# Reordered loads, more staging buffers and finer segment transfers in the forward and backward pass of a strided convolution stem

## The chip, the cores and the metric

The kernel runs on one core of a Trainium2 chip. The metric is the device time of one execution in microseconds (us). The engines are TensorE (PE, with its weight loads as PEld), VectorE (DVE), ScalarE (ACT), GpSimd (POOL) and SyncE (SP); in this kernel SP issues all loads and POOL all stores.

## The reference

The forward pass is a one-dimensional convolution with 31 taps and stride 2, a normalization over the sequence for each channel, and a GELU. The backward pass follows from it for a given `grad_out`.

```
B, T, D, K = 2, 16000, 256, 31            # x [B,T,D], w [K,D,D], all bfloat16
L = (T - K) // 2 + 1                      # 7985
h = sum over i of  x[:, i:i+2*L:2, :] @ w[i]
mu, var over l for each (b, d)
h = (h - mu) / sqrt(var + 1e-5) * gn_gamma + gn_beta
out = gelu(h, approximate=True)
outputs: out, d_x, d_w, d_gamma, d_beta   # the last four by jax.vjp with grad_out
```

Three products of the same size make nearly all of the arithmetic: the forward convolution, the gradient of x, and the gradient of w.

## The kernel before, in words

The kernel is written with a tile framework. Its scheduler places the instructions of each engine from a model of their durations and from the number of buffers in each pool; each engine then executes its own list strictly in order. A buffer that is still being read or stored makes the next writer wait, and everything behind that writer on its engine waits too.

Phase 1, `conv_forward(b)`, runs over 16 tiles of 512 output positions (`LT`) for each of the two batch entries. For each tile, four transposing loads (two halves of the channels, two parities of the stride) bring x with channels on partitions into `xt` buffers, of which there are 16. Then 124 matmuls (L186: 31 taps, two input halves, two output halves) accumulate into two PSUM tiles `acc_f`; ScalarE copies the result into `hT` and sums it and its square (L195, L202). The weights `w_sb` are loaded once at the top, in two transfers (L133), one for each half of the input channels.

Beside the second entry's convolution, the elementwise work of the first one runs, cut into items that are handed out step by step (`elementwise_items`, `run_items`): `bwd_load_go` loads `grad_out` transposed into `gT` (L280, eight large transposing loads), `elementwise_forward` makes the GELU output, `bwd_pass1` multiplies `gT` by the GELU's derivative and sums it, `bwd_pass2` applies the normalization's gradient to `gT`. The forward output and the finished `gT` are turned back to rows in `transpose_and_store`: two PE transposes into a PSUM tile `pt` (L236, two buffers), a ScalarE copy into a staging row (L238), a store by POOL (L239) to the output or to the scratch tensor `gh_dram`. The staging pool `stg` has four buffers for `row` and four for `xrow`.

Phase 2, `conv_backward_x(b)`, makes the gradient of x: for each parity and each chunk of 128 rows, up to 32 matmuls (L451: 16 taps, two halves of d) into `acc_x`, five PSUM buffers, a ScalarE copy to `xrow` (L460) and a store (L461). It needs the weights transposed: `wT_sb` (L480) takes the place of `w_sb` in the same memory, so its load starts when the last forward matmul is done. The elementwise work of the second entry runs beside the first entry's part.

Phase 3 makes the gradient of w. The sequence is cut into 125 blocks of 64 positions, one on each partition (`NG` = 125). Each of four segments (two entries, two halves of a block) holds 32 rows of the gradient per partition in `gseg` and 93 rows of x in `xg`, two buffers each. Both are loaded in three pieces, bounded by gradient rows 8, 20 and 32:

```
s_bounds = [0, min(SH, 8), min(SH, 20), SH]
...
r_hi = min(RW, 2 * (s_hi - 1) + K)
```

`gseg` rows are one load (L542), x rows one load (L550) on 125 partitions, or 124 and a single row (L555) where the last block of x runs out. The taps are taken in groups of eight (`groups`); a group sweeps all 32 rows, 16 matmuls a row (L567), into eight PSUM tiles, and VectorE adds them to the fp32 sum `gw_acc` (L579, L581). At the very end each of 62 half-taps is cast to bfloat16, in turn by VectorE (L587) and ScalarE (L589), and stored by POOL (L590), with four staging buffers `wrow`. The memory of phase 3 is that of phases 1 and 2, so its first load waits for the last work of phase 2.

Of the kernel before, what the change touches and what calls it, by code (L numbers as in the profile page):

```python
# [9 lines left out]
ALU = mybir.AluOpType  # L10
AX = mybir.AxisListType
FP32 = mybir.dt.float32
BF16 = mybir.dt.bfloat16
# [11 lines left out]
def kernel(  # L25
# [13 lines left out]
    nc = tc.nc  # L39
    P = 128  # L40
    B, T, C = x.shape
    K, C2, D = w.shape
    assert C2 == C and C % P == 0 and D % P == 0
    S = 2
    L = (T - K) // S + 1
    assert tuple(grad_out.shape) == (B, L, D)
    NCC = C // P
    NDD = D // P
# [72 lines left out]
    with ExitStack() as ph12:  # L121
# [2 lines left out]
        xtp = ph12.enter_context(tc.tile_pool(name="xtp", bufs=16, side="right"))  # L124
        temps = ph12.enter_context(tc.tile_pool(name="temps", bufs=2, side="right"))
        otp = ph12.enter_context(tc.tile_pool(name="otp", bufs=4, side="right"))
        stg = ph12.enter_context(tc.tile_pool(name="stg", bufs=4, side="right"))
        ps_mm = ph12.enter_context(tc.tile_pool(name="ps_mm", bufs=5, space=bass.MemoryType.PSUM))
        ps_tr = ph12.enter_context(tc.tile_pool(name="ps_tr", bufs=2, space=bass.MemoryType.PSUM))

        w_sb = wpool.tile([P, NCC, K, D], BF16, name="w_sb", tag="w")
        for cc in range(NCC):
            dma_in.dma_start(  # L133
                out=w_sb[:, cc, :, :],
                in_=w[:, cc * P:(cc + 1) * P, :].rearrange("k c d -> c k d"),
            )

        hT = [None] * B
        gT = [None] * B
        wT_holder = [None]  # L140

        def conv_forward(b):
            hT_b = big.tile([P, NDD, GW], BF16, name=f"hT{b}", tag="big")
            hT[b] = hT_b
            for lt in range(NLT):
                l0 = lt * LT
                N = min(LT, L - l0)
                xt = {}
                for cc in range(NCC):
                    for par in range(2):  # L150
                        mmax_p = (K - 1 - par) // 2
                        need = N + mmax_p
                        Wp = ((need + 15) // 16) * 16
                        avail = NU[par] - l0
                        t_xt = xtp.tile([P, LT + 16], BF16, name="xt", tag="xt")
                        if Wp <= avail:
                            dma_in.dma_start_transpose(
                                out=t_xt[:, 0:Wp],
                                in_=x[b, bass.ds(2 * l0 + par, Wp, step=2), cc * P:(cc + 1) * P],
                            )  # L160
                        else:
                            W16 = (need // 16) * 16
                            if W16 > 0:
                                dma_in.dma_start_transpose(
                                    out=t_xt[:, 0:W16],
                                    in_=x[b, bass.ds(2 * l0 + par, W16, step=2), cc * P:(cc + 1) * P],
                                )
                            rem = need - W16
                            if rem > 0:
                                with nc.allow_non_contiguous_dma(reason="xT tail rows"):  # L170
                                    dma_in.dma_start(
                                        out=t_xt[:, W16:need],
                                        in_=x[b, bass.ds(2 * (l0 + W16) + par, rem, step=2),
                                              cc * P:(cc + 1) * P].rearrange("u c -> c u"),
                                    )
                        xt[(cc, par)] = t_xt
                accs = [ps_mm.tile([P, LT], FP32, name="acc_f", tag="acc") for dd in range(NDD)]
                total = K * NCC
                n = 0
                for i in range(K):  # L180
                    par = i % 2
                    m = i // 2
                    for cc in range(NCC):
                        rhs = xt[(cc, par)][:, m:m + N]
                        for dd in range(NDD):
                            nc.tensor.matmul(  # L186
                                accs[dd][:, 0:N],
                                lhsT=w_sb[:, cc, i, dd * P:(dd + 1) * P],
                                rhs=rhs,
                                start=(n == 0),  # L190
                                stop=(n == total - 1),
                            )
                        n += 1
                for dd in range(NDD):
                    nc.scalar.activation(  # L195
                        out=hT_b[:, dd, PADL + l0:PADL + l0 + N],
                        in_=accs[dd][:, 0:N],
                        func=ACT.Copy,
                        accum_out=hsum_part[b][:, dd, lt:lt + 1],
                    )  # L200
                    junk = temps.tile([P, LT], BF16, name="junk_a", tag="junk_a")
                    nc.scalar.activation(  # L202
                        out=junk[:, 0:N],
                        in_=accs[dd][:, 0:N],
                        func=ACT.Square,
                        accum_out=hsq_part[b][:, dd, lt:lt + 1],
                    )
                yield
# [169 lines left out]
        def elementwise_items(b):  # L378
# [1 line left out]
            p1 = bwd_pass1(b)  # L380

            def loader():
                bwd_load_go(b)
                yield "A"

            items.append((loader(), 0.5, False))
# [77 lines left out]
        def n_bx_chunks():  # L464
            return sum(_cdiv(NU[par], P) for par in range(2))

        for _ in conv_forward(0):
            pass
        ew_items = [None] * B
        for b in range(1, B):  # L470
            items = new_sched(elementwise_items(b - 1), lag=1)
# [4 lines left out]
                    run_items(items, (k + 1) / nsteps)  # L476
            run_items(items, 1.0)
        wT_sb = wpool.tile([P, NDD, K, C], BF16, name="wT_sb", tag="w")
        for dd in range(NDD):
            dma_in.dma_start_transpose(  # L480
                out=wT_sb[:, dd, :, :].rearrange("p k c -> p (k c)"),
                in_=w[:, :, dd * P:(dd + 1) * P].rearrange("k c d -> (k c) d"),
            )
        wT_holder[0] = wT_sb
        last = B - 1
        items_last = new_sched(elementwise_items(last), lag=6)
# [23 lines left out]
    with ExitStack() as ph3:  # L510
        accp = ph3.enter_context(tc.tile_pool(name="accp", bufs=1))
        seg = ph3.enter_context(tc.tile_pool(name="seg", bufs=2, side="right"))
        stg3 = ph3.enter_context(tc.tile_pool(name="stg3", bufs=4, side="right"))
        ps_w = ph3.enter_context(tc.tile_pool(name="ps_w", bufs=8, space=bass.MemoryType.PSUM))
        GRP = 8
        groups = [list(range(i0, min(K, i0 + GRP))) for i0 in range(0, K, GRP)]
# [2 lines left out]
        for b in range(B):  # L519
            for h in range(NH):  # L520
# [5 lines left out]
                if nfull < NG:  # L526
                    qb0 = (g_last // 32) * 32
                    r_inv0 = max(0, max_r_last + 1)
                    nc.gpsimd.memset(xg[qb0:qb0 + 32, r_inv0:RW, :], 0.0)  # L529
                s_bounds = [0, min(SH, 8), min(SH, 20), SH]  # L530
                r_prev = 0
                for pi in range(3):
                    s_lo, s_hi = s_bounds[pi], s_bounds[pi + 1]
                    if s_hi <= s_lo:
                        continue
                    r_hi = min(RW, 2 * (s_hi - 1) + K)
                    gsrc = bass.AP(
                        tensor=gh_dram.tensor,
                        offset=gh_dram[b, SH * h + s_lo, 0].offset,
                        ap=[[SB * D, NG], [1, (s_hi - s_lo) * D]],  # L540
                    )
                    dma_in.dma_start(out=gseg[0:NG, s_lo:s_hi, :].rearrange("g s d -> g (s d)"), in_=gsrc)  # L542
                    if r_hi > r_prev:
                        if nfull > 0:
                            src = bass.AP(
                                tensor=x.tensor,
                                offset=x[b, 2 * SH * h + r_prev, 0].offset,
                                ap=[[2 * SB * C, nfull], [1, (r_hi - r_prev) * C]],
                            )
                            dma_in.dma_start(out=xg[0:nfull, r_prev:r_hi, :].rearrange("g r c -> g (r c)"), in_=src)  # L550
                        if nfull < NG:
                            nv = min(max_r_last + 1, r_hi)
                            if nv > r_prev:
# [3 lines left out]
                                    in_=x[b, t0 + r_prev:t0 + nv, :].rearrange("(o r) c -> o r c", o=1),  # L557
                                )
                        r_prev = r_hi
                for grp in groups:  # L560
                    accs = [ps_w.tile([P, NCC, D], FP32, name="acc_w", tag="accw") for _ in grp]
                    total_per_bank = SH * NCC
# [12 lines left out]
                    for ti, i in enumerate(grp):  # L575
                        dst = gw_acc[:, i, :]
                        src_ps = accs[ti][:].rearrange("p k d -> p (k d)")
                        if first_seg:
                            nc.vector.tensor_copy(out=dst, in_=src_ps)  # L579
                        else:  # L580
                            nc.vector.tensor_tensor(out=dst, in0=src_ps, in1=dst, op=ALU.add)  # L581
                first_seg = False
        for i in range(K):
            for cc in range(NCC):
                wrow = stg3.tile([P, D], BF16, name="wrow", tag="wrow")
                if (i * NCC + cc) % 2 == 0:
                    nc.vector.tensor_copy(out=wrow[:], in_=gw_acc[:, i, cc * D:(cc + 1) * D])  # L587
                else:
                    nc.scalar.copy(out=wrow[:], in_=gw_acc[:, i, cc * D:(cc + 1) * D])  # L589
                dma_out.dma_start(out=out_2[i, cc * P:(cc + 1) * P, :], in_=wrow[:])  # L590


# [28 lines left out]
```

## Time and profile before

The median of four runs is 2735.53 us (2733.92 to 2736.33).

| Engine | busy, us | share of the span of 2732.4 us |
|---|---|---|
| PE matmul | 2617.9 | 96% |
| PE weight load | 1965.3 | 72% |
| DVE | 573.2 | 21% |
| ACT | 418.1 | 15% |
| POOL | 321.4 | 12% |

| matmul group | busy, us | count |
|---|---|---|
| forward, L186 | 849.2 | 3968 |
| gradient of x, L451 | 880.5 | 7812 |
| gradient of w, L567 | 870.9 | 7936 |
| transposes, L236 (one of two rows) | 34.8 | 252 |

An engine's busy time counts the stretches in which one of its instructions ran. In lines of groups and waits, `<-` stands between what is written and what is read, or between who waits and who released it; a wait's three numbers are its total, its count and the longest. The columns of a timeline are start, duration, engine, line, operation, tiles and, in brackets, the idle time before it and who ended it. SPq is SP's queue of transfer issues. In windows, the clock that the throttle granted (1.00 is full speed), the mean share of the 16 DMA engines and GB/s stand last.

### The profile page before, as it was taken

How to read it: one execution, taken by the hardware profiler on the slowest of the kernel's cores; microseconds unless marked ns; L12 is line 12 of the kernel's file. 1: busy time of each engine (PE TensorE's matmuls, PEld its weight loads, DVE VectorE, ACT ScalarE, POOL GpSimd, SP SyncE). 2: the span in 40 equal slices, each digit the busy share in tenths (PEclk: the TensorE clock that was granted, in tenths of full speed). 3: DMA queues.
4: the chain of work that ended last, by engine and by line, in shares of the span. 5: the costliest groups of instructions: out<-in, count | busy, mean ns of one | idle time of the engine just before them, and what ended most of it. 6: DMA issues, size and time to landing. Idle time of an engine off the chain costs nothing.

```text
span 2732.4 us, 45468 instructions
## 1 busy us (share of the span) xinstructions
PE 2617.9 (96%) x20220; PEld 1965.3 (72%) x20220; DVE 573.2 (21%) x1547; ACT 418.1 (15%) x1054; POOL 321.4 (12%) x586
## 2 busy tenths in 40 slices
PE   7999999899999799999999999959999999999997
PEld 3444445344445588888888888858888888888886
DVE  0000003946470786660000000000000100010111
ACT  0101013424221544412211111100000000000000
POOL 0000000001011422224311111110000000000112
PEclk9999999999999899999999999989999999999999
DMA  4101012311122401111100000013202001100000
GB/s 100 24 17 24 16 21 41 72 24 40 24 59 49 117 29 35 34 30 59 41 20 21 19 20 21 21 63 108 78 1 100 19 1 50 69 1 1 17 17 30
DMA packets 143088, 104.92 MB, mean 38 GB/s; under 512 B 128836, under 2 KB 128870, under 8 KB 141394
## 3 DMA queue, kind: packets, MB, share of 16 engines
q1 hardware_dynamic: 124652, 65.17, 9.3%
q0 software_dynamic: 18240, 36.85, 4.5%
q8 instruction: 158, 2.59, 0.4%
q14 instruction: 38, 0.31, 0.0%
HBM read 36.04 MB, written 36.82 MB: 27 GB/s over the span
## 4 chain that ended last, share of the span: by engine, by line
PE 35%; issue 22%; POOL 6%; DVE 2%; DMA 1%; ACT 1%; POOLq 0%; ACTq 0%; SPq 0%; DVEq 0%
PE acc_w L567 26%; PE acc_x L451 9%; POOL out_dram L461 3%; POOL gh_dram L239 2%; POOL out_dram L590 1%; DMA xg<-in_x_dram 1%; ACT row L238 0%; DMA gh_dram<-row 0%; PE pt L236 0%; DVE junk_v L336 0%; DVE inner L311 0%; DVE gT L329 0%; DVE inner L257 0%; DVE gw_acc L581 0%; ACT sg L260 0%
## 5 line engine op out<-in xcount | busy, mean ns | idle before, releaser
L567 PE MATMUL acc_w<-gseg,xg 125*128 125x256 bf16 x7936 | 870.9, 273 | 30.9 <-DMA xg<-in_x_dram 30.8
L451 PE MATMUL acc_x<-wT_sb,gT 128*128 128x256 bf16 (+1 forms) x7812 | 880.5, 274 | 4.3 <-issue 4.3
L186 PE MATMUL acc_f<-xt,w_sb 128*128 128x512 bf16 (+1 forms) x3968 | 849.2, 375 | 19.8 <-DMA xt<-in_x_dram 19.8
L567 PEld LDWEIGHTS <-xg 125*128 125x128 bf16 x7936 | 777.5, 98 | 124.2 <-issue 31.3
L451 PEld LDWEIGHTS <-gT 128*128 128x128 bf16 (+1 forms) x7812 | 764.6, 99 | 92.7 <-issue 6.0
L186 PEld LDWEIGHTS <-w_sb 128*128 128x128 bf16 x3968 | 385.1, 98 | 463.5 <-issue 12.4
L461 POOL DMA_DIRECT2D out_dram<-xrow x252 | 136.3, 541 | 650.8 <-ACT xrow L460 583.7
L579 DVE COPY gw_acc<-acc_w 128x512 f32<-128x512 f32 x31 | 18.9, 680 | 841.1 <-PE acc_w L567 841.1
L460 ACT CAST xrow<-acc_x 128x256 bf16<-128x256 f32 (+1 forms) x252 | 93.1, 370 | 592.6 <-PE acc_x L451 574.0
L581 DVE TENSOR_TENSOR gw_acc<-acc_w,gw_acc 128x512 f32<-128x512 f32 x93 | 56.7, 680 | 565.0 <-PE acc_w L567 565.0
L239 POOL DMA_DIRECT2D out_dram<-row x126 | 67.9, 545 | 805.1 <-ACT row L238 792.3
L589 ACT CAST wrow<-gw_acc 128x256 bf16<-128x256 f32 x31 | 12.5, 405 | 900.3 <-DVE gw_acc L581 856.8
L195 ACT ACTIVATE hT<-acc_f 128x512 bf16<-128x512 f32 (+1 forms) x64 | 37.5, 586 | 568.6 <-PE acc_f L186 568.6
L211 DVE TENSOR_REDUCE hsum<-hsum_part 128x2 f32<-128x32 f32 x2 | 0.4, 186 | 516.4 <-ACT hT L195 516.4
L238 ACT COPY row<-pt 128x256 bf16<-128x256 bf16 (+1 forms) x252 | 86.7, 378 | 41.2 <-DMA gh_dram<-row 28.4
L590 POOL DMA_DIRECT2D out_dram<-wrow x62 | 33.4, 543 | 406.6 <-DVE wrow L587 399.1
L239 POOL DMA_DIRECT2D gh_dram<-row x126 | 67.8, 542 | 64.6 <-ACT row L238 61.2
L529 POOL MEMSET xg<- 32x7424 bf16 x2 | 12.6, 6280 | 460.2 <-PE acc_w L567 458.5
L262 DVE TENSOR_TENSOR osl<-z,sg 128x512 bf16<-128x512 bf16 (+1 forms) x64 | 25.0, 414 | 162.9 <-PE pt L236 155.9
L236 PE MATMUL pt<-ident,gT 128*128 128x128 bf16 (+1 forms) x252 | 34.8, 232 | 24.2 <-ACT row L238 23.2
L253 ACT ACTIVATE z<-z 128x512 bf16<-128x512 bf16 (+1 forms) x64 | 39.5, 620 | 118.3 <-DVE z L250 118.0
L236 PEld LDWEIGHTS <-gT 128*128 128x128 bf16 (+1 forms) x252 | 24.3, 104 | 34.9 <-issue 29.6
(74 smaller groups left out, 809.7 us busy)
## 6 DMA issues: line engine op xcount, KB each, us to landing
out_dram<-xrow POOLq DMA_DIRECT2D x248, 64.0 KB, 1.8
out_dram<-row POOLq DMA_DIRECT2D x124, 64.0 KB, 2.1
gh_dram<-row POOLq DMA_DIRECT2D x124, 64.0 KB, 1.8
gseg<-gh_dram SPq DMA_DIRECT2D x8, 750.0 KB
xg<-in_x_dram SPq DMA_DIRECT2D x4, 1500.0 KB
xg<-in_x_dram SPq DMA_DIRECT2D x4, 1488.0 KB
xg<-in_x_dram SPq DMA_DIRECT2D x2, 2812.5 KB
xg<-in_x_dram SPq DMA_DIRECT2D x2, 2790.0 KB
```

The lines of the kernel that those rows point to most:

```text
L186: nc.tensor.matmul(accs[dd][:, 0:N], lhsT=w_sb[:, cc, i, dd * P:(dd + 1) * P], rhs=rhs, start=(n == 0), stop=(n == total - 1),)
L195: nc.scalar.activation(out=hT_b[:, dd, PADL + l0:PADL + l0 + N], in_=accs[dd][:, 0:N], func=ACT.Copy, accum_out=hsum_part[b][:, dd, lt:lt ...
L236: nc.tensor.transpose(out=pt[0:M, dd, :], in_=srcs[dd][:, c0:c0 + M], identity=ident[:])
L238: nc.scalar.copy(out=row[0:M, :], in_=pt[0:M].rearrange("p k d -> p (k d)"))
L239: dma_out.dma_start(out=dram_dst[b, l0 + c0:l0 + c0 + M, :], in_=row[0:M, :])
L253: nc.scalar.activation(out=z2[:, 0:N], in_=z[:, 0:N], func=ACT.Square)
L451: nc.tensor.matmul(acc[0:Mu, 0:C], lhsT=gT_b[:, dd, PADL + u0 - m:PADL + u0 - m + Mu], rhs=wT_sb[:, dd, i, :], start=(n == 0), stop=(n == ...
L460: nc.scalar.copy(out=xrow[0:Mu, :], in_=acc[0:Mu, 0:C])
L461: dma_out.dma_start(out=out_1[b, bass.ds(2 * u0 + par, Mu, step=2), :], in_=xrow[0:Mu, :])
L567: nc.tensor.matmul(accs[ti][:, cc, :], lhsT=xg[0:NG, 2 * s + i, cc * P:(cc + 1) * P], rhs=gseg[0:NG, s, :], start=(cnt[ti] == 0), stop=(cn ...
L581: nc.vector.tensor_tensor(out=dst, in0=src_ps, in1=dst, op=ALU.add)
L590: dma_out.dma_start(out=out_2[i, cc * P:(cc + 1) * P, :], in_=wrow[:])
```

## The change

The change touches every place where loads, staging or stores stand next to the matmuls, and leaves the matmuls as they are.

- The first tile's activations are loaded ahead of the weights, and the weights come tap by tap in 31 loads.
- Activation tiles are requested three tiles ahead by a list.
- The first entry's gradient is loaded after step 8 of the first convolution.
- `stg` has 12 buffers of each kind instead of 4.
- The transposed weights come in eight loads: four groups of up to eight taps, two halves each.
- Each segment of phase 3 is loaded in six pieces, bounded by rows 4, 8, 14, 20, 26 and 32; a piece has only the x rows that the first group of taps needs, and each load is split at partition 112.
- In the last segment, VectorE writes the sum straight to a bfloat16 row, which is stored, so that the closing loop of casts goes.

```diff
-        stg = ph12.enter_context(tc.tile_pool(name="stg", bufs=4, side="right"))
+        stg = ph12.enter_context(tc.tile_pool(name="stg", bufs=12, side="right"))
...
-        for cc in range(NCC):
-            dma_in.dma_start(
-                out=w_sb[:, cc, :, :],
-                in_=w[:, cc * P:(cc + 1) * P, :].rearrange("k c d -> c k d"),
-            )
+        def load_w():
...
+            for i in range(K):
+                dma_in.dma_start(
+                    out=w_sb[:, :, i, :],
+                    in_=w[i].rearrange("(cc c) d -> c cc d", c=P),
+                )
...
+        XT_LEAD = 3
...
+        def prefetch_xt(upto_idx):
+            for idx in range(min(upto_idx + 1, len(conv_order))):
+                key = conv_order[idx]
+                if key not in xt_q:
+                    xt_q[key] = load_xt(*key)
+                    if not w_loaded[0]:
+                        load_w()
...
+                idx = conv_order.index((b, lt))
+                prefetch_xt(idx + XT_LEAD)
+                xt = xt_q[(b, lt)]
...
             def loader():
-                bwd_load_go(b)
+                if b > 0:
+                    bwd_load_go(b)
                 yield "A"
...
-        for _ in conv_forward(0):
-            pass
+        for k, _ in enumerate(conv_forward(0)):
+            if k == 8:
+                bwd_load_go(0)
...
-        for dd in range(NDD):
-            dma_in.dma_start_transpose(
-                out=wT_sb[:, dd, :, :].rearrange("p k c -> p (k c)"),
-                in_=w[:, :, dd * P:(dd + 1) * P].rearrange("k c d -> (k c) d"),
-            )
+        TG = 8
+        for i0 in range(0, K, TG):
+            i1 = min(K, i0 + TG)
+            for dd in range(NDD):
+                dma_in.dma_start_transpose(
+                    out=wT_sb[:, dd, i0:i1, :].rearrange("p k c -> p (k c)"),
+                    in_=w[i0:i1, :, dd * P:(dd + 1) * P].rearrange("k c d -> (k c) d"),
+                )
...
-        stg3 = ph3.enter_context(tc.tile_pool(name="stg3", bufs=4, side="right"))
+        stg3 = ph3.enter_context(tc.tile_pool(name="stg3", bufs=16, side="right"))
...
-                s_bounds = [0, min(SH, 8), min(SH, 20), SH]
+                s_bounds = sorted(set([0] + [min(SH, v) for v in (4, 8, 14, 20, 26)] + [SH]))
...
-                    r_hi = min(RW, 2 * (s_hi - 1) + K)
-                    gsrc = bass.AP(
-                        tensor=gh_dram.tensor,
-                        offset=gh_dram[b, SH * h + s_lo, 0].offset,
-                        ap=[[SB * D, NG], [1, (s_hi - s_lo) * D]],
-                    )
-                    dma_in.dma_start(out=gseg[0:NG, s_lo:s_hi, :].rearrange("g s d -> g (s d)"), in_=gsrc)
+                    r_hi = RW if s_hi == SH else min(RW, 2 * (s_hi - 1) + GRP)
+                    PG = (NG // 16) * 16
+                    for p0, p1 in ((0, PG), (PG, NG)):
+                        gsrc = bass.AP(
+                            tensor=gh_dram.tensor,
+                            offset=gh_dram[b, SB * p0 + SH * h + s_lo, 0].offset,
+                            ap=[[SB * D, p1 - p0], [1, (s_hi - s_lo) * D]],
+                        )
+                        dma_in.dma_start(out=gseg[p0:p1, s_lo:s_hi, :].rearrange("g s d -> g (s d)"), in_=gsrc)
...
+                        for p0, p1 in ((0, PG), (PG, nfull)):
...
-                            dma_in.dma_start(out=xg[0:nfull, r_prev:r_hi, :].rearrange("g r c -> g (r c)"), in_=src)
+                            dma_in.dma_start(out=xg[p0:p1, r_prev:r_hi, :].rearrange("g r c -> g (r c)"), in_=src)
...
+                last_seg = (b == B - 1) and (h == NH - 1)
...
-                        else:
+                        elif not last_seg:
                             nc.vector.tensor_tensor(out=dst, in0=src_ps, in1=dst, op=ALU.add)
+                        else:
+                            for cc in range(NCC):
+                                wrow = stg3.tile([P, D], BF16, name="wrow", tag="wrow")
+                                nc.vector.tensor_tensor(out=wrow[:], in0=accs[ti][:, cc, :],
+                                                        in1=gw_acc[:, i, cc * D:(cc + 1) * D], op=ALU.add)
+                                dma_out.dma_start(out=out_2[i, cc * P:(cc + 1) * P, :], in_=wrow[:])
...
-                if (i * NCC + cc) % 2 == 0:
-                    nc.vector.tensor_copy(out=wrow[:], in_=gw_acc[:, i, cc * D:(cc + 1) * D])
-                else:
-                    nc.scalar.copy(out=wrow[:], in_=gw_acc[:, i, cc * D:(cc + 1) * D])
-                dma_out.dma_start(out=out_2[i, cc * P:(cc + 1) * P, :], in_=wrow[:])
```

## The prediction

> **What bounds the kernel now.** I read the page's busy line first, then the waits of PE, then the timeline around each of the long ones. The two lines below are the busy line of the page and the matmul line of its forty slices.
>
> ```profile
> PE 2617.9 (96%) x20220; PEld 1965.3 (72%) x20220; DVE 573.2 (21%) x1547; ACT 418.1 (15%) x1054; POOL 321.4 (12%) x586
> PE   7999999899999799999999999959999999999997
> ```
>
> The reader sees that TensorE is the bound: 2617.9 of 2732.4 us. The change keeps all 20220 matmuls, so at most the other 114.5 us can go, with the time in which PE runs at half clock after a pause. The dips are where that lies: slices 1, 8, 14, 27 and 40. The waits of PE put numbers to it:
>
> ```profile
> PE pt L236 <- ACT row L238: 41.2, 28, 7.8
> PE acc_w L567 <- DMA xg<-in_x_dram: 30.8, 1, 30.8
> PE acc_f L186 <- DMA xt<-in_x_dram: 19.8, 2, 19.4
> PE acc_x L451 <- issue: 4.3, 1, 4.3
> ```
>
> That is 96.1 us in 32 waits. The last matmul starts at 2716.0, so some 16 us of tail make most of the rest. Now each place on the timeline: the start, the handover to the weight gradient, the second sweep's start, the tail.
>
> ```profile
> 1.96 6.09 SPq L133 DMA_DIRECT2D w_sb<-in_w_dram  x2
> 19.44 1.01 PE L186 MATMUL acc_f<-xt,w_sb 128*128 128x512 bf16 x2 [19.44 <-DMA xt<-in_x_dram]
> ...
> 886.63 17.57 SPq L480 DMA_TRANSPOSE wT_sb<-in_w_dram  x2
> 911.30 0.42 PE L451 MATMUL acc_x<-wT_sb,gT 128*128 128x256 bf16 x1
> ...
> 1817.33 0.34 SPq L542 DMA_DIRECT2D gseg<-gh_dram  x1
> 1817.72 0.28 SPq L550 DMA_DIRECT2D xg<-in_x_dram  x1
> 1845.34 5.07 PE L567 MATMUL acc_w<-gseg,xg 125*128 125x256 bf16 x23 [30.82 <-DMA xg<-in_x_dram]
> ...
> 2719.76 2.13 POOL L590 DMA_DIRECT2D out_dram<-wrow  x4 [36.05 <-DVE wrow L587]
> 2728.10 0.54 POOL L590 DMA_DIRECT2D out_dram<-wrow  x1 [0.29 <-ACT wrow L589]
> ```
>
> The first activations queue behind the whole weight load. At the handover PE waits 28 us for a first piece of 3.39 MB (gseg 8 rows, xg 45 rows of 512 B on 125 partitions): 121 GB/s. The windows say why it is slow (busy columns, then clock, DMA share, GB/s):
>
> ```profile
> 1821.00:1824.00 3.00, 0.00 (x0) 0.00 (x0) 0.00 (x0) 0.00 (x0) 2.84 (x1) 0.50 0.37 155
> 1833.00:1836.00 3.00, 0.00 (x0) 0.00 (x0) 0.00 (x0) 0.00 (x0) 0.00 (x0) 0.50 0.34 146
> 10.00:12.00 2.00, 0.00 (x0) 0.07 (x1) 0.00 (x0) 0.00 (x0) 0.00 (x0) 1.00 1.06 291
> ```
>
> Only a third of the 16 DMA engines moves it, while the weight load at the start keeps all busy. And behind PE's wait for row copies stand these:
>
> ```profile
> ACT row L238 <- DMA gh_dram<-row: 28.4, 32, 3.6
> ACT xrow L460 <- DMA out_dram<-xrow: 11.8, 1, 11.8
> DVE gT L329 <- DMA gT<-in_grad_out_dram: 8.8, 2, 7.1
> ```
>
> ScalarE waits for one of four staging rows to be stored, and VectorE waits for gradient transposes that arrive late.
>
> [...] 5/16 is 0.31, and the share is 0.28 to 0.37. [...] the trace's row stores land 1.8 to 2.1 us after issue. [...] after a pause PE falls to half clock[...]: 0.50 from 1821, 6 us after the last matmul, and 23 matmuls in 5.07 us after it, against 2.5 us at the mean of 0.11.
>
> **The change part by part.**
>
> *Start.* Activations first, then 31 tap loads. Two small loads end by 1.8; four transposes at 1.1 to 1.2 us each (row of L157: 1108 minimum) reach 6.5; the first tap (131 KB, 0.45 us at 291 GB/s) is issued in about 0.4 us and lands some 2 us later: first matmul at 9.2 instead of 19.44. Later taps arrive every 0.45 us and feed four matmuls (0.85 us), so PE is not starved. The next activation tiles are issued from 20.5 and land by 28, needed at about 37. Gain 10.2 us (8 to 12). The lead of 3 tiles changes nothing: the 16 buffers already let the queue run four tiles ahead.
>
> *Gradient load at step 8.* The 8.8 us VectorE wait pushes back ScalarE, whose row copies stand behind its elementwise work, and PE sits 7.8 us at 497 to 504.8, then some 4 us at half clock (2 us lost). Eight transposes of 2.4 us on the queue near 240 us hide under a lead of three tiles, 80 us. The built order has its row copies still behind elementwise work, so some small waits stay: gain 8 us (4 to 10).
>
> *Twelve staging rows, weights in eight transposes.* The built program's order now has PE issue 80 matmuls of acc_x before it needs the last weight piece; before, five. The last piece still lands near 906 (same bytes from 886.6). But ScalarE now paces: after the forward sweep's end at 888 it has 46 row copies (0.37 plus a gap, 0.40: 18.4), about 12 elementwise calls of 0.62 (7.4), 5 xrow copies (1.9), table loads and the root (2.9): 30.6 us, so the transposes end at 918.6. Before they ended at 935.9, with 34 more acc_x done (3.7 us). That is 13.6. Against it, transposes now stand one or two matmuls apart (0.13 + 0.19 us each against 0.40 on ScalarE), costing 1.4 us in the 14 before the sweep's end. ScalarE was busy only 31 of 50 us there before, so I don't trust it to run gapless: gain 10 us (3 to 15). In the second batch's burst near 1300 the denser order gives back what the rows save: 0.
>
> *xrow.* POOL stops 12 us at 1215 behind the two 2-byte-strided parameter stores; four xrow buffers fill, and PE loses 4.3 us and then 2.8 (25 matmuls in 5.5 us). Twelve buffers at one per 3.3 us are 39 us of slack: gain 6.5.
>
> *Handover.* First piece: gseg 4 rows, xg 14 rows: 1.15 MB in four DMAs[...]. At 121 × 16/5 = 387 GB/s that is 3.0 us; at the weight load's 290 it is 4.0. Four issues of 0.38, and 2 us to land: first matmul at 1822.8 (1822 to 1825.5) instead of 1845.3. Then 192 KB per step s, which PE works off in 16 × 0.11 = 1.75 us: 110 GB/s, well under the rate. Gain 22.5 (18 to 23). The half-clock start stays, as 8 us of pause is still enough for it.
>
> *Tail.* Before, adds of 0.61 each for 7 taps, then 14 casts and stores through four rows: the last issue at 2728.1, 13 us after the first add. Now 14 half-size adds (estimate 0.34 each: half of 0.61 plus a margin) feed POOL at 0.543: first issue 2715.5, last 2715.5 + 13 × 0.543 = 2722.6. Gain 5.5 (4 to 6). The extra adds in the earlier groups lie beside PE.
>
> Sum: 10.2 + 8 + 10 + 6.5 + 22.5 + 5.5 = 62.7; 2735.5 − 62.7 = 2673.
>
> **Rivals.** *R1, ScalarE and POOL take over in the transposes:* the denser order speaks for it, POOL's 0.54 per store as well; that 46 copies only take 18 us speaks against. The 18 us of the gradient load and staging parts vanish, 4 more lost: 2695. *R2, the handover stays long:* 24 to 29 small DMAs per segment on one queue[...]. If they run at the old 121 GB/s, the first piece still takes 9.5 us and lands at about 1829, and then 121 GB/s against the 110 that PE needs leaves no room, say 3 us of waits: gain 13, total 2682. *R3, everything overlaps:* ScalarE gapless, all PE waits for rows gone: 63 + 15 = 2658. *R4, slower:* tap and piece loads become serial at some 3 us each. Twenty pieces for the first group then take 60 us against the 44 PE needs, the taps 93 against 27, about 80 lost, minus the gains elsewhere: 2750. The issue durations of 0.34 us speak against it.
>
> **How the numbers follow.** Forecast 0.60, R1 0.18, R2 0.10, R3 0.08, R4 0.04. The time is the forecast's, 2673. The range takes in R2, most of R1, and the upper ends of start and transposes in the forecast and R3: 2654 to 2700. Faster 0.95, same 0.01, slower 0.04.
>
> **What would show it.** Right: first acc_f near 9; no PE wait over 3 us near 500; acc_x going from 893 on, transposes done near 919; no issue gap near 1225; acc_w 8 to 9 us after the last acc_x with a DMA share near 1; last store issued 7 us after the first. Wrong: PE waiting for row copies over 30 us in all, or acc_w stopping for gseg or xg within its first group.

## The result and the profile after

The changed kernel takes 2679.26 us (median of eight runs, 2676.4 to 2682.08) against 2735.81 us for the kernel before (twelve runs, 2733.67 to 2737.74). The ratio is 0.9794, with a 95% interval of 0.9784 to 0.9804: 56.5 us less, where 62.7 was forecast.

The busy line and the matmul line of the slices, from the page of the changed kernel:

```profile
PE 2615.0 (98%) x20220; PEld 1963.4 (73%) x20220; DVE 566.9 (21%) x1547; ACT 404.3 (15%) x1023; POOL 321.1 (12%) x586
PE   8999999999999899999999999989999999999998
```

PE does the same 20220 matmuls in nearly the same busy time (2617.9 us before). The span fell from 2732.4 to 2675.3 us, and the time that is not PE's from 114.5 to 60.3. The waits of PE in the changed kernel say what is left of it:

```profile
PE pt L262 <- ACT row L264: 15.7, 8, 4.6
PE acc_w L601 <- DMA xg<-in_x_dram: 11.0, 1, 11.0
PE acc_f L212 <- DMA w_sb<-in_w_dram: 9.8, 1, 9.8
PE acc_x L478 <- DMA wT_sb<-in_w_dram: 6.9, 6, 2.2
PE acc_x L478 <- issue: 3.5, 2, 3.0
```

The wait for row copies fell from 41.2 to 15.7, the handover from 30.8 to 11.0, the start from 19.8 to 9.8. A new row has come, the wait for pieces of the transposed weights. The gap that the profile gives to "issue", time in which PE waits for nothing that the profile shows, is still there. The places where these waits stand, on the changed kernel's timeline:

```profile
9.76 10.61 PE L212 MATMUL acc_f<-xt,w_sb 128*128 128x512 bf16 x41 [9.76 <-DMA w_sb<-in_w_dram]
...
490.83 0.37 PE L262 MATMUL pt<-ident,osl 128*128 128x128 bf16 x2 [4.63 <-ACT row L264]
...
876.44 1.15 PE L478 MATMUL acc_x<-wT_sb,gT 128*128 128x256 bf16 x5 [2.23 <-DMA wT_sb<-in_w_dram]
...
905.48 0.29 PE L262 MATMUL pt<-ident,gT 128*49 128x128 bf16 x2
...
960.68 0.37 PE L262 MATMUL pt<-ident,osl 128*128 128x128 bf16 x2 [4.56 <-ACT row L264]
...
1787.07 0.83 SPq L575 DMA_DIRECT2D gseg<-gh_dram  x2
1787.96 0.77 SPq L583 DMA_DIRECT2D xg<-in_x_dram  x2
1795.25 16.95 PE L601 MATMUL acc_w<-gseg,xg 125*128 125x256 bf16 x141 [10.99 <-DMA xg<-in_x_dram]
...
2663.41 4.72 DVE L619 TENSOR_TENSOR wrow<-acc_w,gw_acc 128x256 bf16<-128x256 f32 x14 [43.74 <-PE acc_w L601]
2664.12 7.43 POOL L621 DMA_DIRECT2D out_dram<-wrow  x14 [38.04 <-DVE wrow L619]
```

To compare traces I cut each at the start of certain matmuls (the first of a group, the 400th acc_x, and so on). The second pair of columns is a repetition of both kernels, from the experiments below, where the kernel before takes 8.6 us less. Times are us.

| stage | before | changed | before, again | changed, again |
|---|---|---|---|---|
| to the first acc_f | 19.4 | 9.8 | 19.3 | 9.5 |
| to the end of the forward sweeps | 866.9 | 861.1 | 865.9 | 863.4 |
| to the 400th acc_x | 82.3 | 68.4 | 81.2 | 66.7 |
| to the 2000th acc_x | 183.8 | 187.6 | 185.4 | 188.0 |
| to the 2800th (parameter stores) | 98.7 | 97.7 | 91.6 | 91.9 |
| to the 3400th (second row burst) | 81.1 | 77.3 | 80.2 | 77.3 |
| last acc_x to first acc_w | 31.1 | 11.3 | 30.9 | 11.0 |
| last acc_w to the end | 16.4 | 10.9 | 16.4 | 10.9 |

The stages left out (the last 4400 acc_x, the rest of phase 3) make 1.5 us together. In the first pair the gains are 9.7 at the start, 5.8 in the forward sweeps, 13.9 in the overlap behind them, of which the next stage gives 3.8 back, 1.0 at the parameter stores, 3.8 in the second burst, 19.8 at the handover and 5.5 in the tail. Two things were not in the forecast: one stage is slower than before, and the parameter-store stage, of which 6.5 us were expected, shows next to nothing.

### The profile page after: what moved, and what is told of

Read it like the earlier page. It is cut to its first block, busy times and chain, and to the rows that moved or that the text cites. A ratio compares the mean times of both kernels' runs of the same rounds, so it can differ in the third digit from the quotient of the medians.

```text
span 2675.3 us, 45553 instructions
## 1 busy us (share of the span) xinstructions
PE 2615.0 (98%) x20220; PEld 1963.4 (73%) x20220; DVE 566.9 (21%) x1547; ACT 404.3 (15%) x1023; POOL 321.1 (12%) x586
## 3 DMA queue, kind: packets, MB, share of 16 engines
q1 hardware_dynamic: 135536, 65.18, 11.3%
q8 instruction: 158, 2.59, 0.4%
## 4 chain that ended last, share of the span: by engine, by line
PE 33%; issue 16%; POOL 3%; DMA 0%; ACT 0%; DVE 0%; POOLq 0%; SPq 0%; DVEq 0%; ACTq 0%
PE acc_w L601 32%; POOL out_dram L488 3%; PE acc_x L478 1%; DMA xg<-in_x_dram 0%; POOL gh_dram L265 0%; PE pt L262 0%; ACT row L264 0%; DVE wrow L619 0%; POOLq L488 0%; POOL out_dram L621 0%; DVE gw_acc L613 0%; DMA out_dram<-xrow 0%; SPq L575 0%; POOLq L654 0%; DVEq L654 0%
## 5 line engine op out<-in xcount | busy, mean ns | idle before, releaser
L478 PEld LDWEIGHTS <-gT 128*128 128x128 bf16 (+1 forms) x7812 | 764.7, 99 | 100.1 <-issue 13.4
L615 DVE TENSOR_TENSOR gw_acc<-acc_w,gw_acc 128x512 f32<-128x512 f32 x62 | 37.8, 680 | 396.3 <-PE acc_w L601 396.3
L619 DVE TENSOR_TENSOR wrow<-acc_w,gw_acc 128x256 bf16<-128x256 f32 x62 | 20.9, 412 | 196.3 <-PE acc_w L601 196.3
L398 DVE SCALAR_TENSOR_TENSOR gT<-y,bbcoef,tq 128x512 bf16<-128x512 bf16 (+1 forms) x64 | 46.4, 727 | 0.0
L262 PE MATMUL pt<-ident,osl 128*128 128x128 bf16 (+1 forms) x252 | 30.6, 222 | 14.6 <-ACT row L264 13.4
```

The source lines that it names most:

```text
L398: nc.vector.scalar_tensor_tensor(out=gseg, in0=y[:, 0:N], scalar=bbcoef[b][:, dd:dd + 1], in1=tq[:, 0:N], op0=ALU.mult, op1=ALU.add)
L478: nc.tensor.matmul(acc[0:Mu, 0:C], lhsT=gT_b[:, dd, PADL + u0 - m:PADL + u0 - m + Mu], rhs=wT_sb[:, dd, i, :], start=(n == 0), stop=(n == ...
```

## The experiments

The study ran on three chips (0, 5 and 6 in the record, which names none for the first pair), where the kernel before takes 2725.8 to 2731.1 us. So single totals are not set against the 2679.26 above; I read the stages. Traces of the same code differ by some 3 us in the forward sweeps (860.8 to 864.3), so nothing smaller is read there.

### The two kernels again

> The changed kernel itself, beside the next two on one chip, for the comparison of their traces: a ratio to the kernel before near 0.979, as on the first chip, or up to 0.983 if the pause at the parameter stores, which differed by several us from run to run in the same code, is part of what the chips differ by.

> The kernel before itself, for its trace on this chip: 31 us at the handover, 82 us from the end of the forward sweep to the 400th matmul of acc_x, 16 us of tail, as on the first chip; the pause at the parameter stores may be shorter than 4.3 us.

The changed kernel took 2673.42 us (four runs) against 2727.24 for the kernel before, ratio 0.9805 [0.9792, 0.9819]. The kernel before, run alone, took 2725.79. Their stages are the right half of the table: everything repeats within 3 us, except the parameter-store stage. That stage is 98.7 and 91.6 us for the same code of before, 97.7 and 91.9 for the same changed code. Between the two kernels of one pair it hardly differs. The eight traces of the study that keep the old stores, on all three chips, have 91.6 to 93.1 us, so whether the 97.7 and 98.7 of the first pair belong to its chip or to chance stays open.

### The parameter stores

The forecast held that four xrow buffers filled while POOL was held up by the two stores of 256 two-byte pieces each. The changed kernel has twelve, and its timeline still shows this:

```profile
1183.16 0.72 POOL L539 DMA_DIRECT2D out_dram<-gbet_bf  x1
...
1190.75 0.37 ACT L487 CAST xrow<-acc_x 128x256 bf16<-128x256 f32 x1 [2.29 <-PE acc_x L478]
1197.57 0.37 PE L478 MATMUL acc_x<-wT_sb,gT 128*128 128x256 bf16 x1 [2.97 <-issue]
...
1198.93 0.37 ACT L487 CAST xrow<-acc_x 128x256 bf16<-128x256 f32 x1 [7.81 <-remote]
1201.73 0.54 POOL L265 DMA_DIRECT2D out_dram<-row  x1 [12.19 <-DMA out_dram<-ggam_bf]
```

After the two stores, ScalarE stands still for 7.8 us with no releaser on this core ("remote"), of which some 2.9 are its usual wait for the next chunk, and PE for 2.97 plus 0.54 us with none at all. Both go on within 1.4 us of each other, while POOL still waits. A buffer cannot be what ScalarE waits for: with one xrow every 3.3 us, twelve last 39 us. Nor can PE be out of accumulators, of which it has five: the pause of 8 us is 2.4 chunks. So I stored the two vectors as rows of 256 bytes, in the changed kernel (e1) and in the one before (e7):

```diff
...
-        dma_out.dma_start(out=out_3.rearrange("(k p) -> p k", p=P), in_=ggam_bf[:])
-        dma_out.dma_start(out=out_4.rearrange("(k p) -> p k", p=P), in_=gbet_bf[:])
...
+        pt_gb = ps_tr.tile([P, NDD, P], BF16, name="pt_gb", tag="pt")
+        nc.tensor.transpose(out=pt_gb[0:2 * NDD, 0, :], in_=gb_bf[:], identity=ident[:])
+        gb_row = const.tile([P, P], BF16, name="gb_row")
+        nc.scalar.copy(out=gb_row[0:2 * NDD, :], in_=pt_gb[0:2 * NDD, 0, :])
+        dma_out.dma_start(out=out_3.rearrange("(k p) -> k p", p=P), in_=gb_row[0:NDD, :])
+        dma_out.dma_start(out=out_4.rearrange("(k p) -> k p", p=P), in_=gb_row[NDD:2 * NDD, :])
```

> The changed kernel with the gradients of gamma and beta turned to rows by one PE transpose and stored as 256-byte rows, instead of 256 two-byte pieces each. Theory F (the two-byte stores hold up the transfers that refill the engines' instructions, so PE and ScalarE stop at once): the 3.5 us of PE idle without a releaser near 1195 and the half clock after it go, POOL no longer waits 12 us for a parameter store, the last acc_x ends 5 to 7 us earlier, total about 2673. Theory B (PE stops because its PSUM buffers or xrow buffers are full): POOL's wait also goes, so the time is the same as with F; but then the changed kernel's 12 xrow buffers should have removed the stall already. Theory N (the stall has nothing to do with these stores): 2679 and the idle stays.

> The kernel before with the parameter gradients stored as 256-byte rows. Theory F: the 4.3 us of PE idle near 1222 and the half clock after it go, 6 to 7 us in all: 2729. Rival: 2735 and the idle stays, or moves to where four xrow buffers are full.

e1 took 2673.41 us and e7 2728.61, one run each. The totals show no gain: the changed kernel's repetition took 2673.42, and the kernel before 2726.57 on e7's chip. The stage is 91.0 us in e1 and 91.3 in e7, 0.9 and 0.3 below the repetitions, so the 5 to 7 us that were expected didn't come where the pause was short to begin with.

The edit moves the stores as well as reshaping them. The built order puts the new transpose behind the last matmul of phase 2, so the rows are stored some 600 us later than the strided pieces (those start at 1182.46 and 1183.16 in the changed kernel):

```profile
1781.37 0.53 POOL L540 DMA_DIRECT2D out_dram<-gb_row  x1
```

So e1 and e7 show what happens without the strided stores in the middle of phase 2. They don't tell the form of the stores from their place. The stretch of ten microseconds after the stores, in the windows of the changed kernel and then of e1:

```profile
1190.00:1200.00 10.00, 6.50 (x52) 5.08 (x50) 0.00 (x0) 0.74 (x2) 0.00 (x0) 0.87 0.06 7
```

```profile
1190.00:1200.00 10.00, 10.00 (x94) 8.96 (x93) 0.00 (x0) 1.12 (x3) 2.85 (x6) 1.00 0.14 41
```

In the changed kernel PE loses 3.5 us and then runs below full clock, down to 0.65 in the 6 us after 1200; in e1 it works all the time at full clock, and POOL issues stores throughout. The DMA view of the same 26 us shows what else is different. First the changed kernel, then e1:

```profile
q8 instruction: 1, 0.02, 1.4%
out_dram<-xrow POOLq DMA_DIRECT2D x6, 64.0 KB, 15.4
out_dram<-row POOLq DMA_DIRECT2D x4, 64.0 KB, 14.7
```

```profile
q8 instruction: 2, 0.03, 0.6%
out_dram<-xrow POOLq DMA_DIRECT2D x8, 64.0 KB, 1.8
out_dram<-row POOLq DMA_DIRECT2D x4, 64.0 KB, 3.0
```

Behind the strided stores a row takes 14.7 to 15.4 us to land instead of 1.8 to 3.0; e1's rows of 256 bytes landed 1.6 us after issue. No run tells the mechanism. The one packet of the instruction queue took 1.4% of 16 engines for 26 us, or 5.8 us; in e1 each took 1.2 (0.6% × 16 × 26 / 2). So a late packet of this queue would explain why two engines stop together with no releaser, which is a guess: the profile names the queue, not who waits for it. The other traces support it in part. In all ten with the strided stores the instruction packet due behind them took 2.6 to 11.2 us (seven traces) or began only 25 to 26 us after the one before it, where 12 to 16 are usual (e2, e3, e4); in the four with rows none took over 1.6 there. But in five of the ten (both pairs and e5) PE goes on only 3 to 9 us after that packet has ended, and in nine of the ten POOL goes on within 2.1 us of PE. With twelve buffers the profile names nothing for ScalarE's stop in two traces and the landing of a row store in five. So whether that packet is what stops PE, or all of them wait for the traffic of the stores to pass, isn't settled.

What is shown: with the strided stores, all ten traces, the first pair's among them, have an issue wait of PE's acc_x, from 0.2 to 4.3 us, and 4.8 to 12.2 us between two of ScalarE's xrow copies behind the stores, where 3.3 are usual. With the rows at the end (e1, e7 and two later runs), none of four has an issue wait, and no two copies there are more than 4.0 us apart. The size differs from trace to trace in the same code. The number of buffers is not what decides PE's part of it: with four it is 4.3, 0.2 and 0.8 us (both traces of the kernel before and e4), with twelve 0.8 to 3.5.

### Four staging buffers, weights in two loads, gradient loaded late

Three kernels undo one part each of the changed one: four buffers again (e4), `wT_sb` in two loads (e5), the first entry's gradient loaded by the items again (e6).

```diff
-        stg = ph12.enter_context(tc.tile_pool(name="stg", bufs=12, side="right"))
+        stg = ph12.enter_context(tc.tile_pool(name="stg", bufs=4, side="right"))
```
```diff
-        TG = 8
+        TG = K
```
```diff
-                if b > 0:
-                    bwd_load_go(b)
+                bwd_load_go(b)
...
-        for k, _ in enumerate(conv_forward(0)):
-            if k == 8:
-                bwd_load_go(0)
+        for _ in conv_forward(0):
+            pass
```

> The changed kernel with 4 staging rows of each kind again. Theory S (the rows' share of the gain lies around the start of the second sweep): ScalarE waits for row stores 20 to 28 us in all again, the built order spreads the transposes wider again, the first entry's last transposes end 5 to 10 us later relative to the end of the forward sweep, total 2685 to 2690. Rival W (the weights in eight loads did it all, rows are only waited for while the weights are missing anyway): total within 2 us of 2679.

> The changed kernel with the transposed weights in two loads again. Theory W: PE has only 5 matmuls of acc_x to do before the second load lands near 893, 75 fewer than with eight loads, so 8 us are lost: total 2687. Rival S (ScalarE's row copies set the pace until 905 anyway): total within 2 us of 2679.

> The changed kernel with the first entry's gradient loaded by the elementwise list again, beside the second convolution. Theory G: VectorE waits 8 to 9 us for the gradient, ScalarE falls back, PE loses 7 to 8 us near 490 instead of 4.6, plus the half clock after it: total 2682 to 2685. Rival (the wait for row copies near 490 comes from the order of ScalarE's list and not from the load): total 2679.

| us | total | forward sweeps | to 400th acc_x | to 2000th | parameter stores | second burst |
|---|---|---|---|---|---|---|
| changed, again | 2673.4 | 863.4 | 66.7 | 188.0 | 91.9 | 77.3 |
| e4, four buffers | 2681.8 | 863.7 | 70.5 | 187.2 | 92.0 | 83.0 |
| e5, two loads | 2677.2 | 861.2 | 77.7 | 183.6 | 93.1 | 77.3 |
| e6, gradient late | 2675.0 | 865.5 | 67.5 | 187.1 | 92.3 | 77.3 |

*Rows (e4).* ScalarE's waits and PE's waits in e4, one line of each:

```profile
ACT row L264 <- DMA gh_dram<-row: 27.0, 35, 2.6
```

```profile
PE pt L262 <- ACT row L264: 27.7, 22, 4.6
```

ScalarE waits for staging rows as it did in the kernel before (28.4), against 2.3 to 2.6 us in the two traces of the changed kernel; PE waits 12 us more. Of that, 2 to 4 us are in the first burst and 5.7 in the second (83.0 against 77.3). In the parameter-store stage e4 is no slower than its neighbours, although ScalarE does wait there 10.1 us for one of four xrow: the xrow buffers are worth nothing here. The rows also decide when the first entry's transposes are done: 48.1 us after the forward sweeps in e4, 32.8 to 34.6 in the two traces of the changed kernel.

*Pieces of the transposed weights (e5).* With two loads the stage to the 400th acc_x is 9.3 to 11.0 us longer than in the two traces of the changed kernel, and the next is 4.0 to 4.4 shorter, so the eight loads are worth 5.3 to 6.6, of the 8 expected. The second number is not a cost of theirs. PE's timeline in the changed kernel has a wait of 4.56 us at 960.68 (above), in the second of the two stages. E5 has it as well, but earlier, ahead of its 400th acc_x at 948.7:

```profile
945.74 0.37 PE L262 MATMUL pt<-ident,osl 128*128 128x128 bf16 x2 [4.50 <-ACT row L264]
```

In the kernel before there are four shorter waits of 1.27 to 2.59 us between 928 and 988, 7.9 us in all, of which only the last is behind its 400th acc_x (968.6). In the changed kernel the row copy stands on ScalarE behind the second entry's elementwise chain, where a ScalarE instruction at 954.38 waited 4.66 us for VectorE. The reading is that PE now gets there before that chain is done; no run tests it. The long wait costs clock as well: 0.83 on the mean from 950 to 970.

*Gradient load (e6).* The sweeps are 1.2 to 4.7 us longer than in the traces with the early load (860.8 to 864.3), and the wait that the load was to end is back, in VectorE's waits and PE's longest:

```profile
DVE gT L355 <- DMA gT<-in_grad_out_dram: 7.9, 2, 6.6
```

```profile
PE pt L262 <- ACT row L264: 18.2, 8, 6.9
```

The longest wait is 6.9 us, where 7 to 8 were expected, against 4.6: the early load takes 2.3 us off it. The 4.6 that remain (490.83 above) are not the load's: in that stretch ScalarE's own list has two elementwise calls of 0.63 us, each waiting on VectorE (the first for 4.93 us), and then the forward tile's copies, before it comes to the row copy.

### The handover: division, piece size, number of engines

Three kernels: one load of 125 partitions instead of 112 and 13 (e2), the old three pieces but divided at 112 (e3), and a division at 100 (e9), with a DMA share of 0.56 to 0.62 in the wait, or some ten of the 16 engines.

```diff
-                    for p0, p1 in ((0, PG), (PG, NG)):
+                    for p0, p1 in ((0, NG),):
...
-                        for p0, p1 in ((0, PG), (PG, nfull)):
+                        for p0, p1 in ((0, nfull),):
```
```diff
-                s_bounds = sorted(set([0] + [min(SH, v) for v in (4, 8, 14, 20, 26)] + [SH]))
+                s_bounds = [0, min(SH, 8), min(SH, 20), SH]
...
-                    r_hi = RW if s_hi == SH else min(RW, 2 * (s_hi - 1) + GRP)
+                    r_hi = min(RW, 2 * (s_hi - 1) + K)
```
```diff
-                    PG = (NG // 16) * 16
+                    PG = 100
```

> The changed kernel with each segment load undivided at 125 (or 124) partitions, pieces as they are. Theory K (the engine count follows from the partition count): DMA share near 0.31 and 120 to 146 GB/s at the handover; the first piece of 1.15 MB needs about 9.5 us instead of 4.8, so acc_w starts about 16 us after the last acc_x instead of 11, and 121 GB/s against a need of 110 may leave short waits in the first group: total 2684 to 2690. Rival (dividing partitions does nothing, the small first piece did it all): 11 us, total 2679.

> The changed kernel with the three old pieces per segment and the old x rows, each still divided at partition 112. Theory K: 3.39 MB at about 245 GB/s take 13.8 us, acc_w starts about 20 us after the last acc_x (31 before, 11 changed): total 2688. Rival (the division does nothing): 31 us, total 2699.

> The changed kernel with the loads divided at partition 100 instead of 112[...]. Theory M (the 240 GB/s that the first piece reached is a bound outside the DMA engines): each engine runs at up to 27 GB/s again[...], acc_w starts 11 to 12 us after the last acc_x. Theory E (each engine is limited to about 15.6 GB/s with such transfers):[...] acc_w starts about 15 us after.

| us | total | last acc_x to first acc_w | first acc_w to the 511th after it |
|---|---|---|---|
| before, again | 2725.8 | 30.9 | 58.5 |
| e3, large pieces, divided | 2688.7 | 24.7 | 57.7 |
| e2, small pieces, not divided | 2681.0 | 14.7 | 63.4 |
| e9, small, divided at 100 | 2676.9 | 14.4 | 58.3 |
| changed, again | 2673.4 | 11.0 | 58.6 |

Windows inside the wait, in the changed kernel, then e2, then e9 (DMA share and GB/s are the last two numbers):

```profile
1790.00:1793.00 3.00, 0.00 (x0) 0.00 (x0) 0.00 (x0) 0.00 (x0) 3.00 (x1) 0.50 1.00 289
1793.00:1796.00 3.00, 0.75 (x4) 0.58 (x5) 0.00 (x0) 0.00 (x0) 0.58 (x1) 0.50 1.03 252
```

```profile
1787.00:1790.00 3.00, 0.00 (x0) 0.00 (x0) 0.00 (x0) 0.00 (x0) 0.74 (x1) 0.50 0.32 134
```

```profile
1788.00:1791.00 3.00, 0.00 (x0) 0.00 (x0) 0.00 (x0) 0.00 (x0) 1.11 (x1) 0.50 0.62 207
```

The share is 1.00 to 1.03 in the changed kernel, 0.32 in e2 and 0.62 in e9: times 16, as much as 16, 5 and 10 engines. The rate grows more slowly than that: 134 GB/s on 5, 207 on 10, 252 to 289 on 16, or 26.8, 20.7 and 16 to 18 per engine. So neither theory of e9 holds as written. Its wait of 14.4 us is near the 15 of a fixed limit per engine, but by this count its engines ran at 20.7 GB/s, above the 15.6 of that limit and below the 27 of the other, both of them estimates. Of the 19.9 us between 30.9 and 11.0, small pieces alone make 16.2 (e2) and the division alone 6.2 (e3); they overlap by 2.5. Without the division the small pieces aren't enough for what follows. In e2 PE stops for xg a second time, as PE's waits say:

```profile
PE acc_w L601 <- DMA xg<-in_x_dram: 17.8, 2, 14.4
```

The second stop is 3.4 us, and the first 511 matmuls take 4.8 us longer. e3 came later than expected, 24.7 us instead of 20: from its first issue to its first matmul 209 GB/s moved for 21.6 us, 4.5 MB, where the first piece is 3.39, so the pieces behind it shared the rate. What the division changes is the share: 0.31 to 0.33 for the undivided 125 partitions of e2, 1.00 to 1.03 for the same pieces divided at 112. The division is worth 3.7 + 4.8 = 8.5 us, near the 7.6 between the totals, which are single runs on two chips.

### A version with more taken out

e10 puts together e1's rows, the first two taps ahead of the activations (even parity first), pieces bounded at 2, 6, 10, 15, 20 and 26, and every second store of the tail issued by SP. e11 is the same with all tail stores on POOL.

```diff
-            for cc in range(NCC):
-                for par in range(2):
+            for par in range(2):
+                for cc in range(NCC):
...
+                        load_w(0, 2)
                     xt_q[key] = load_xt(*key)
...
+                        load_w(2, K)
...
-                s_bounds = sorted(set([0] + [min(SH, v) for v in (4, 8, 14, 20, 26)] + [SH]))
+                s_bounds = sorted(set([0] + [min(SH, v) for v in (2, 6, 10, 15, 20, 26)] + [SH]))
...
+                                q_out = dma_out if cc == 0 else dma_in
```

> The changed kernel with the parameter gradients stored as rows, the first two weight taps loaded ahead of the activations and both channel halves of one parity first, a first segment piece of 2 rows instead of 4 (0.77 MB instead of 1.15), and the last stores shared between POOL and SP. By the theory that each place is an independent wait on the path: start 1.5 us earlier, no pause at the parameter stores (1 to 6), handover 1.6 shorter, tail 3 shorter: 7 to 12 us below the changed kernel. Rival: the start and the handover are bound by something that the sizes don't move[...], and only stores and tail give: 4 to 9.

> The combined kernel with all last stores on POOL again, as in the changed kernel. In the combined kernel POOL's closing drain lasted 9.6 us, 8 us past the last transfer's landing, and took back what the second queue had saved. Theory D (sharing the stores between two queues makes the drain long): the tail from the last matmul is 10.9 us as in the changed kernel instead of 14.1, and the ratio to the kernel before falls from 0.9794 to about 0.978. Rival (the drain's length is chance, or comes from the parameter rows): the tail stays near 14 us and the ratio near 0.979.

e10 took 2671.65 us (five runs), ratio 0.9794 [0.9781, 0.9807]: 1.8 us below the changed kernel on the same chip, where 7 to 12 were expected and the rival had 4 to 9. Its start is 6.4 us and its handover 9.0, but its tail is 14.1. In the chain that ended last, these are its last pieces (start, us, what):

```profile
2658.99 0.53 POOL out_dram L625
2659.52 0.53 POOLq L658
```

The last store is issued early, but the span ends at 2669.9, 9.9 us after the last piece. In the changed kernel that closing stretch is 3.7 us, in e11 3.4. Each is one trace, so what SP's share of the stores does to the close isn't settled; e11 leaves it out, and its tail is 10.5 us (10.9 expected). e11 took 2669.69 us (five runs) against 2731.13, ratio 0.9771 [0.9758, 0.9784], the lowest of all. Its interval only touches the changed kernel's (0.9784 to 0.9804) and lies below the repetition's (0.9792 to 0.9819), so the step beyond it is small: it is the best version found. PE's waits in e11:

```profile
PE pt L263 <- ACT row L265: 16.6, 9, 4.6
PE acc_w L604 <- DMA xg<-in_x_dram: 8.9, 1, 8.9
PE acc_x L479 <- DMA wT_sb<-in_w_dram: 7.4, 5, 2.4
PE acc_f L213 <- DMA xt<-in_x_dram: 6.6, 3, 5.8
```

The issue wait is gone, the start and the handover are shorter, and the rows' wait is as it was. The earlier start isn't seen further on: the forward sweeps end at 872.5 us, no earlier than the 870.9 to 874.1 of the traces with the changed kernel's start.

## Why the prediction was right, and where its sum was off

The direction and the main mechanisms held, and 2679.3 lies in the range of 2654 to 2700. The sum was 6 us too large. By its own steps:

- **Start.** Forecast 9.2, gain 10.2; measured 9.76, gain 9.7. PE isn't starved by later taps: its only wait for `w_sb` is this first one. The 2 us to land had been read from POOL's stores (1.8 to 2.1 us) and were used for SP's loads. No run undoes this part alone; the timeline carries the reading.
- **Gradient load.** Gain of 8 forecast; 5.8 in the forward sweeps in the first pair, 2.5 in the second. The term was mis-sized: I gave the whole 7.8 us wait to the load, and e6 shows 2.3 us of it to be the load's, while 4.6 stay with the order of ScalarE's list, of which I had expected only "some small waits".
- **Rows and transposed weights.** Gain of 10 forecast; 13.9 less 3.8 is 10.1, and in the second pair 14.5 less 2.6 is 11.9. Its 918.6 for the end of the transposes is counted from the kernel before, whose sweeps end near 887; in the changed kernel they end at 871.2 and the last two transposes start at 905.5. From the end of the sweeps to the end of the transposes it is 34.6 us, against the 30.6 summed for ScalarE and 49.6 in the kernel before, whose last two are these:

```profile
935.88 0.29 PE L236 MATMUL pt<-ident,gT 128*49 128x128 bf16 x2
```

So ScalarE was 4 us slower than summed, and the transposes are done 15 us sooner; 13.9 of this is there at the 400th acc_x and 3.8 go again in the next stage. That the sum fits 10 is luck to this extent, since no step named what is given back: PE has one wait of 4.6 us near 961 where the kernel before had four short ones. e5 has it with two loads (4.50), e6 with the late gradient (4.54) and e4 with four buffers (3.56), so none of these edits makes it alone. What does is left open.

- **Second burst.** Forecast 0; measured 3.8 (2.9 in the second pair), and e4 gives 5.7 for the staging buffers. I took the denser order to eat what the rows save; it doesn't.
- **xrow.** Gain of 6.5 forecast; measured 1.0 and, in the second pair, −0.3. This step failed in its cause. POOL's stop and PE's gap were read as one chain through full xrow buffers. The gap stays with twelve buffers, is no larger with four (e4), and disappears when the strided stores go from that place (e1, e7).
- **Handover.** 22.5 forecast, 19.8 measured. The reading held, with a small first piece and a DMA share of 1.00 to 1.03 where it was 0.27 to 0.37. That the divided loads would keep all engines busy was an estimate, which no trace of the kernel before showed. The mis-sized term is the first piece's transfer, for which I scaled 121 GB/s with the engines to 387 and counted no other traffic. From the first issue at 1787.07 to the first matmul at 1795.25, 220 GB/s moved on average, 1.80 MB, of which the first piece is 1.15 (as worked out in the prediction); the rest belongs to the pieces issued behind it, already in flight. The forecast gave it 5.5 us from first issue to first matmul; it took 8.2.
- **Tail.** 5.5 forecast, 5.5 measured: the 14 adds take 4.72 us, 0.337 each, and POOL's 14 issues 7.43. This part too no run undoes alone, so the direct adds and the 16 buffers aren't told apart.

That the total came within 6 us is in part luck, since the misses have both signs. In the first pair 5.5 at xrow, 2.7 at the handover, 2.2 at the gradient load and 0.5 at the start, less 3.8 from the second burst and 1.5 in the stages left out of the table, make 5.6; the rest of the 6 is the spread of single runs around their median. R1 is refuted by the transposes' end, 34.6 us after the sweeps instead of 49.6; R2 needed the old rate, and R4 serial pieces, which neither the windows nor the issues show. R3's gapless ScalarE fails at 490 and 961.

## What to carry to other kernels

Before a wait is put down to a full buffer, count how long the buffers last; if the wait is shorter than that, more of them will not help (here ScalarE stood for 7.8 us with 39 us of buffers), and an engine that stops with no releaser may be stopped by traffic from elsewhere. A load that keeps only part of the DMA engines busy (a share of 0.32 on 125 partitions here, of 1.00 on 112 and 13) is worth dividing where somebody waits for it (8.5 us here), but price it by a rate measured with as many engines busy (252 to 289 GB/s), not by scaling up (387). Small pieces ahead of a wait give most where the first piece is what is waited for (16.2 of 19.9 us here); when a consumer arrives earlier, ask which other chain it now meets unfinished.

## What the runs showed of the hardware

- The rate of these loads grew more slowly than the DMA share: 134 GB/s at 0.32 (e2), 207 at 0.62 (e9), 252 to 289 at 1.00 to 1.03 (changed) in the handover's windows.
- Two stores of 256 two-byte pieces each held POOL for 12.2 us in the changed kernel's trace, and ScalarE stopped for 7.8 us and PE for 3.5 with no releaser; in the same kernel's second trace PE lost 0.8. As rows of 256 bytes, stored some 600 us later, they landed in 1.6 us and stopped no engine in e1.
